# Rounding weights while the first batch is filtered: another interleaving in a spectral mixing + SwiGLU kernel

## The chip, the cores and the metric

The kernel runs on one core of a Trainium2 chip. The metric is the device time of one execution in microseconds (us). The engines are TensorE (PE, with its weight loads PEld), VectorE (DVE), ScalarE (ACT), GpSimd (Pool) and SyncE (SP, which here only issues DMAs; ACT issues some too). Each engine works through its own instructions strictly in the program's order, so an instruction that waits holds up all that stand behind it on its engine.

## The reference, cut to what matters

```python
batch, seq, dim = (8, 3008, 256)          # n_tokens = 24064, d_model = 256, d_ff = 1536
def _attn_ref(x, filt_r, filt_i):
    X = np.fft.rfft(x, axis=1)
    Y = X * (filt_r + 1j * filt_i)[None, :, :]
    return np.fft.irfft(Y, n=x.shape[1], axis=1).astype(np.float32)

def _moe_ref(x, w_gate, w_val, w_out):    # weights are float64
    g = x @ w_gate
    silu = g * (1.0 / (1.0 + np.exp(-g)))
    return (silu * (x @ w_val) @ w_out).astype(np.float32)
```

A real FFT along the sequence, a product with a filter, the inverse FFT, then a gated feed-forward block on every token. The three weight matrices come as float64, so each value arrives as two 32-bit words.

## The kernel before

The FFT is a product of two smaller DFTs (47 x 64) done as matmuls: stage 1 (`wpa`/`pa`), a transposition for the first batch (`wpt`), stage 2a (`wpb`: second DFT), the product with the filter on DVE and Pool, stage 2b (`wpc`: back), a way through DRAM (`d`), stage 3 (`wpd`/`pd`: last inverse DFT). Then 4 chunks of tokens x 3 groups of the hidden width make 12 steps of a batch, 96 in all. In a step a fast (Winograd-like) scheme makes the hidden values from sums of the sequence (`y_t`) and sums of the weights (`wt_t`, in the first batch `lent` for group 1): products `wk` (tokens P and Q of the schedule), `wa` (A, B) and `we` (E), then Silu and the product (`h`), sums of h on Pool, and the projection (`wA`, `wF`, `wG`) of the step before. In the first batch the order is three chunks for group 0 (steps 0 to 2), three for group 1 (3 to 5), three for group 2 (6 to 8), since the weights come ready one group after another. Spectral work of the next chunk or batch is mixed into the steps.

The change is in how the weights are prepared during the first batch. There are 36 halves of weight blocks (12 to each group: 8 for the hidden layer, 4 for the projection). Each half is loaded as raw 32-bit words and turned from float64 into float32 by DVE and ACT (bit masks and a scale), then Pool multiplies and combines. The numbers at the right are the line numbers by which the profile names them.

```python
    NRAW = 2
    N_EARLY = 15                       # these halves lie in places not yet used otherwise
    def load_weights(i):
        ...
        else:
            raws[i] = rpool.tile([128, 2, 128, 2], U32, ..., tag="raw", bufs=NRAW)
        queue = nc.sync if i < N_EARLY else nc.scalar
        pin(queue.dma_start(out=raws[i], in_=weights[i][0]))            # L272

    def round_half(i):
        ...
        w = rpool.tile([128, 2, 128], FP32, ..., tag="w", bufs=2)
        pin(v.tensor_scalar(out=man, in0=high, ...bitwise_and))         # L285 DVE
        pin(nc.scalar.activation(out=w, in_=man, func=AF.Copy, ...))    # L287 ACT
        yield
        pin(v.tensor_scalar(out=pw, in0=high, ...shift, and))           # L289 DVE
        pin(nc.scalar.activation(out=pf, in_=pw, func=AF.Relu, ...))    # L292 ACT
        load_weights(i + NRAW - 1)
        yield
        pin(nc.scalar.activation(out=pf, in_=pf, func=AF.Relu, ...))    # L296 ACT
        pin(nc.scalar.activation(out=pw, in_=pf, func=AF.Copy, ...))    # L297 ACT
        yield
        pin(v.scalar_tensor_tensor(out=pw, in0=raw[..1], in1=pw, ...))  # L300 DVE
        yield
        pin(v.scalar_tensor_tensor(out=w, in0=raw[..0], in1=w, ...))    # L304 DVE
        yield
        # then products and sums on Pool: L312 (projection), L323, L324, L224, L227
```

`preparing()` puts the yields of all halves in one line, with a half's Pool part inside the next half, and one weight combination a tick behind a group's last hidden half. `preparation.tick(step, n)` takes n pieces of it. Where ticks stand in the first batch:

```python
        for u in range(8):
            spec.stage1_first(u)
            if u > 3:
                preparation.tick(0, 2 + u % 2)
        ...
        for u in range(N_TWO + lag):                  # N_TWO = 12, lag = 3
            if u < N_TWO:
                spec.turn(u + 2)
                run(spec.stage2a(u))                  # matmul, 3 DVE products, 1 Pool addition
                preparation.tick(0, 1 + u % 2)
                spec.real_part(u + 1)                 # ACT copies the filter's real part, L564
                preparation.tick(0)
            if u >= lag:
                run(spec.stage2b(u - lag))
        ...                                           # loads for stage 3 (all rows)
        preparation.tick(0, 14)
        warm()                                        # idle matmuls that keep the clock up
        for step in range(4):
            run(spec.stage3(0, step))
    for d in (2, 1, 3):                               # sums of the sequence at distance d
        combine_sequence(spec.y[0], d, nc.vector if d == 1 else nc.gpsimd)
    ...
            for place, token in enumerate(SCHEDULE):
                if b == 0 and this and place * TICKS % len(SCHEDULE) < TICKS:   # TICKS = 24 a step
                    preparation.tick(step)
```

In stage 2a, the three DVE products of a tile (L548 or L551, L552, L555) read the matmul's result in PSUM; L555 releases the Pool addition `pt + qt` (L224, `room`).

Of the kernel before, what the change touches and what calls it, by code (L numbers as in the profile page):

```python
# [58 lines left out]
NH = 4  # L59
# [85 lines left out]
def kernel(  # L145
# [58 lines left out]
    off_t = cpool.tile([128, 1], FP32)  # L204
    top_t = cpool.tile([128, 1], FP32)
    nc.vector.memset(off_t, -896.0)
    nc.vector.memset(top_t, 255.0)
# [52 lines left out]
    raws = {}  # L260
    NRAW = 2
    N_EARLY = 15

    def load_weights(i):
        if i in raws or i >= len(weights):
            return
        if i < N_EARLY:
            raws[i] = early_raw(i)
        else:
            raws[i] = rpool.tile([128, 2, 128, 2], U32, name=f"raw_{i}", tag="raw", bufs=NRAW)  # L270
        queue = nc.sync if i < N_EARLY else nc.scalar
        pin(queue.dma_start(out=raws[i], in_=weights[i][0]))  # L272

    def round_half(i):
# [4 lines left out]
        pw = rpool.tile([128, 2, 128], U32, name=f"pw_{i}", tag="pw", bufs=3)  # L279
        w = rpool.tile([128, 2, 128], FP32, name=f"w_{i}", tag="w", bufs=2)  # L280
        man = w.bitcast(U32)
# [4 lines left out]
                            op0=ALU.bitwise_and))  # L286
        pin(nc.scalar.activation(out=w, in_=man, func=AF.Copy, scale=2.0 ** -20, bias=1.0))  # L287
        yield
        pin(v.tensor_scalar(out=pw, in0=high, scalar1=20, scalar2=0x7FF,  # L289
                            op0=ALU.logical_shift_right, op1=ALU.bitwise_and))  # L290
        pf = pw.bitcast(FP32)
        pin(nc.scalar.activation(out=pf, in_=pw, func=AF.Relu, bias=off_t))  # L292

        load_weights(i + NRAW - 1)
        yield
        pin(nc.scalar.activation(out=pf, in_=pf, func=AF.Relu, bias=top_t, scale=-1.0))  # L296
        pin(nc.scalar.activation(out=pw, in_=pf, func=AF.Copy, scale=-(2.0 ** 23),  # L297
# [11 lines left out]
        if use == "proj":  # L309
            j, l = at  # L310
            dst = wo_t[:, j]
            pin(e.tensor_tensor(out=dst[:, ts(l, 2), :], in0=w, in1=pf, op=ALU.mult))  # L312
            if l:
                b11, b12, b21, b22, t1, t2, t4 = [dst[:, i] for i in range(7)]
                pin(sub(e, t1, b12, b11))
                pin(sub(e, t2, b22, t1))
                pin(sub(e, b12, b22, b12))
                pin(sub(e, t4, b21, t2))
            return
# [3 lines left out]
        pin(e.tensor_tensor(out=y, in0=w[:, 1], in1=pf[:, 1], op=ALU.mult))  # L323
        pin(e.tensor_tensor(out=x if KS[i] else u, in0=x, in1=pf[:, 0], op=ALU.mult))  # L324
        if KS[i] == -1:
            pin(sub(e, u, x, y))
        elif KS[i]:
            pin(add(e, u, x, y))
            if KS[i] == 2:
                pin(add(e, u, u, y))  # L330

    def combine_weights(g, i, j):

        d = j - i
        wt_f = weights_of(0, 0, g).rearrange("p s z f -> p s (z f)")
        m = wt_f[:, SLOT[f"A{i}{j}"]]
        ui, uj, yi, yj = [wt_f[:, SLOT[f"{p}{q}"]] for p in "PQ" for q in (i, j)]
        if d == 1:
            pin(negated_sum(m, ui, uj))
        else:  # L340
            pin(add(nc.vector, m, ui, uj))
            pin(nc.scalar.mul(m, m, -1.0 / d))
        pin(sub(nc.gpsimd, wt_f[:, SLOT[f"B{i}{j}"]], yi, m))
        pin(add(nc.gpsimd, wt_f[:, SLOT[f"E{i}{j}"]], yj, m))
# [9 lines left out]

    def preparing():


        late = None
        for i in range(len(weights)):
            use, *at = weights[i][1]  # L360
            if use == "hid":
                window = (0, 0, 3)[at[0]], (0, 3, 6)[at[0]]
            else:
                window = 0 if at[0] < 2 * JB else 3, (1, 4, 7)[at[0] // JB]
            half = round_half(i)
            for n in range(5):
                yield window
                if n == 2 and late:
                    next(late, None)
                next(half)  # L370
            late = half
            if use == "hid" and at[1:] == [BLOCKS[-1], 1]:
                yield window
                next(late, None)
                for pair in PAIRS_USED:
                    yield window
                    combine_weights(at[0], *pair)
        yield window
        next(late, None)

    class Preparation:
        def __init__(self):
            self.steps = preparing()
            self.window = next(self.steps)

        def tick(self, step, n=1):
            for _ in range(n):
                if self.window and self.window[0] <= step:
                    self.window = next(self.steps, None)

        def finish(self, step):
            while self.window and self.window[1] <= step:
                self.window = next(self.steps, None)

    preparation = Preparation()
    TICKS = 24

# [20 lines left out]
    class Spectral:  # L418
# [58 lines left out]

        def load_t4(self, k, i):
            if self.b == 0 and k == 0:

                t = f0[0:NK, ts(i, NH), :]
                for r in (slice(0, NK - 16), slice(NK - 16, NK)):
                    self.load(out=t[r], in_=self.d2_rows[r, ts(i, NH), :])
            else:
                t = t4pool.tile([NK, NH, C], FP32, name=f"t4_{self.b}_{k}_{i}", tag="t4")
                self.load(out=t, in_=self.d2_rows[:, ts(2 * k + i, NH), :])
            self.t4[k, i] = t
# [78 lines left out]
        def stage2b(self, u):  # L566
# [8 lines left out]
            pin(nc.scalar.copy(out=g, in_=ps))  # L575
            queue = nc.scalar if self.b else nc.sync
            pin(queue.dma_start(out=self.twos(self.d2, u), in_=g))
# [39 lines left out]

    def combine_sequence(y, d, v=nc.gpsimd):

        n = 4 - d  # L620
        yb, yv = y[:, 0:4], y[:, 4:8]
        first = SUM[f"A0{d}"]
        pa, pb, pe = [y_t[:, first + 6 * e:first + 6 * e + n] for e in range(3)]
        pin(add(v, pa, yv[:, 0:n], yv[:, d:4]))
        if d == 1:
            pin(sub(v, pe, pa, yb[:, 0:n]))
            pin(add(v, pb, pa, yb[:, d:4]))
            return
        for dst, src, f in ((pe, yb[:, 0:n], -d), (pb, yb[:, d:4], d)):
            pin(nc.scalar.mul(dst, src, float(f)))  # L630
            pin(add(v, dst, dst, pa))
# [155 lines left out]
    with tc.tile_pool(name="start", bufs=1) as spool0:  # L787
# [22 lines left out]
        def early_raw(i):  # L810
            t = wt_t[:, spare[i]:spare[i] + 2].rearrange("p s z f -> p (s z f)") if i < 8 else \
                wo_f[:, JB * 7 * 128 + 512 * (i - 8):JB * 7 * 128 + 512 * (i - 7)]
            return t.bitcast(U32).rearrange("p (b f two) -> p b f two", b=2, two=2)

        unit_t = spool0.tile([128, 128], FP32, name="unit")
        pin(nc.scalar.dma_start(out=unit_t, in_=unit_dram.ap()))
        pin(nc.vector.memset(zero, 0.0))
        idle(zero, [bank("idle") for _ in range(5)], 512)
        pin(nc.sync.dma_start(out=wf_t, in_=wf_dram.ap()))
# [6 lines left out]
        for u in range(8):  # L826
# [3 lines left out]
            if u > 3:  # L830
                preparation.tick(0, 2 + u % 2)
        for i in range(8, N_EARLY):
# [4 lines left out]
        for u in range(N_TWO + lag):  # L837
            if u < N_TWO:
                spec.turn(u + 2)
                run(spec.stage2a(u))  # L840
                preparation.tick(0, 1 + u % 2)
                spec.real_part(u + 1)
                preparation.tick(0)
            if u >= lag:
                run(spec.stage2b(u - lag))
        for i in range(2):
            spec.load_t4(0, i)
        for i in range(2):
            spec.load_t4(1, i)
        following = Spectral(1)  # L850
        for u in range(2):
            following.load_x(u)
        preparation.tick(0, 14)
        warm()
        for step in range(4):
            run(spec.stage3(0, step))
    for d in (2, 1, 3):
        combine_sequence(spec.y[0], d, nc.vector if d == 1 else nc.gpsimd)

# [52 lines left out]
    def chore(step, token, f, *args):  # L912
        chores.setdefault((step, token), []).append((f, args))

    for step in range(NT):
        for d, token in ((2, "Q2"), (1, "A01"), (3, "Q3")):
# [10 lines left out]
    for g, step in ((0, 1), (1, 3), (2, 6)):  # L927
        for piece, token in enumerate(("B02", "B12", "A23", "B23")):
            chore(step, token, keep_weights, g, piece)

    for b in range(B):
# [33 lines left out]
        for step in range(NCHUNK * NG + (b == B - 1)):  # L965
# [17 lines left out]
            for place, token in enumerate(SCHEDULE):  # L983
                if b == 0 and this and place * TICKS % len(SCHEDULE) < TICKS:
                    preparation.tick(step)
# [64 lines left out]
```

## Time and profile before

| | |
|---|---|
| time, median of 3 runs | 3009.26 us (3007.68 to 3009.94) |
| span of the profiled execution | 3004.9 us |
| PE busy | 2938.8 us (98%) |
| DVE, ACT, Pool busy | 65%, 54%, 53% |
| mean granted clock of TensorE | 0.991 |

"Busy" counts time in which an engine has an instruction in work; PE can be busy and yet slow when the granted clock is below 1. The last part of a line of a timeline, in brackets, is the time that the engine stood idle before the instruction, and what ended it. A table of stretches has, in this order: the stretch in us from the start, its length, busy time (and instructions) of PE, PEld, DVE, ACT and Pool, the mean granted clock, the DMA engines' busy share, and GB/s. The first chunk's steps begin at 97.0, 136.7, 171.4, 208.3, 252.4, 283.3, 322.6 us (the first `f<-wk` of each).

### The profile page before, as it was taken

The numbers are of one execution on the slowest core, as the hardware profiler recorded it, in microseconds if no ns is written. First come the engines' busy times: TensorE is split into PE (matmuls) and PEld (weight loads), VectorE is DVE, ScalarE is ACT, GpSimd is POOL, SyncE is SP. The second block draws the span as 40 slices with busy tenths as digits, with TensorE's granted clock in tenths as the row PEclk, the third lists the DMA queues.
The fourth block names the chain that finished last, engine by engine and source line by source line (L and its number), as shares of the span: only waits on it lengthen the run. The fifth ranks groups of instructions, "written<-read, shape, count | busy, mean of one in ns | idle before, by whom it ended". The sixth has DMA issues, their size and how long they took to land.

```text
span 3004.9 us, 57645 instructions
## 1 busy us (share of the span) xinstructions
PE 2938.8 (98%) x20286; PEld 2838.2 (94%) x20286; DVE 1939.4 (65%) x4380; ACT 1615.8 (54%) x4207; POOL 1583.5 (53%) x1763
## 2 busy tenths in 40 slices
PE   7798999999999999999999999999999999999999
PEld 5787899999999999999999999999999999999999
DVE  7766776566765666557665576655776566766665
ACT  5566445555555555555555545555545555555554
POOL 3675465445645555545545555545555445554453
PEclk9899999999999999999999999999999999999999
DMA  7467684656655656456655575556664566644442
GB/s 204 130 208 256 226 281 155 191 186 205 198 170 175 215 180 209 154 191 204 197 177 186 172 230 178 182 175 193 200 211 158 184 193 195 199 160 145 139 136 89
DMA packets 217082, 558.60 MB, mean 186 GB/s; under 512 B 29872, under 2 KB 107552, under 8 KB 216512
## 3 DMA queue, kind: packets, MB, share of 16 engines
q1 hardware_dynamic: 167354, 481.13, 50.1%
q10 hardware_dynamic: 40512, 49.89, 5.0%
q0 software_dynamic: 8928, 23.89, 2.6%
q8 instruction: 163, 2.67, 0.4%
q14 instruction: 125, 1.02, 0.1%
HBM read 459.73 MB, written 95.05 MB: 185 GB/s over the span
## 4 chain that ended last, share of the span: by engine, by line
PE 89%; POOL 1%; DMA 1%; DVE 1%; ACT 1%; issue 0%; ACTq 0%; SPq 0%; DVEq 0%; POOLq 0%
PE wa L679 23%; PE wA L758 16%; PE wk L679 15%; PE we L679 12%; PE wG L758 8%; PE wF L758 4%; PE pd L587 3%; PE pa L499 3%; PE pc L571 2%; PE pb L539 2%; DMA raw<-in_moe_w_val_dram 0%; POOL h L227 0%; DVE o L224 0%; DMA lent<-in_filt_r_dram 0%; POOL wt_t L224 0%
## 5 line engine op out<-in xcount | busy, mean ns | idle before, releaser
L679 PE MATMUL wa<-y_t,wt_t 128*128 128x188 f32 x4464 | 884.2, 324 | 12.0 <-POOL wo_t L227 3.9
L679 PEld LDWEIGHTS wa<-y_t,wt_t 128*128 128x128 f32 x4464 | 733.6, 191 | 37.6 <-issue 18.4
L224 POOL TENSOR_TENSOR h<-h 128x376 f32<-128x376 f32 x190 | 183.3, 985 | 790.1 <-DVE h L726 790.1
L758 PE MATMUL wA<-wo_t,h 128*128 128x128 f32 x4608 | 580.0, 276 | 6.8 <-DVE o L224 5.0
L758 PEld LDWEIGHTS wA<-wo_t,h 128*128 128x128 f32 x4608 | 564.6, 192 | 22.2 <-issue 11.5
L679 PE MATMUL wk<-y,wt_t 128*128 128x188 f32 x2976 | 571.1, 325 | 4.2 <-ACT f L694 2.7
L227 POOL TENSOR_TENSOR h<-h 128x376 f32<-128x376 f32 x570 | 555.0, 995 | 0.5
L679 PEld LDWEIGHTS wk<-y,wt_t 128*128 128x128 f32 x2976 | 482.0, 191 | 29.8 <-issue 19.8
L227 DVE TENSOR_TENSOR we<-we,m 128x376 f32<-128x376 f32 x576 | 318.7, 556 | 196.7 <-PE we L679 140.4
L679 PE MATMUL we<-y_t,wt_t 128*128 128x188 f32 x2232 | 432.4, 323 | 0.0
L679 PEld LDWEIGHTS we<-y_t,wt_t 128*128 128x128 f32 x2232 | 370.5, 190 | 0.0
L227 POOL TENSOR_TENSOR D<-f,f 128x376 f32<-128x376 f32 x288 | 280.2, 986 | 118.7 <-ACT f L694 118.0
L231 DVE SCALAR_TENSOR_TENSOR y<-wk,c 128x376 f32<-128x376 f32 x480 | 245.2, 543 | 143.6 <-ACT we L710 88.8
L714 ACT COPY m<-wa 128x376 f32<-128x376 f32 x576 | 271.6, 472 | 88.4 <-PE wa L679 87.5
L758 PE MATMUL wG<-wo_t,h 128*128 128x128 f32 x2304 | 288.3, 275 | 0.6 <-DVE o L224 0.6
L721 ACT ACTIVATE g<-wa 128x188 f32<-128x188 f32 x576 | 187.6, 326 | 187.8 <-PE wa L679 181.0
L758 PEld LDWEIGHTS wG<-wo_t,h 128*128 128x128 f32 x2304 | 281.4, 192 | 0.8 <-DVE o L224 0.8
L721 ACT ACTIVATE u<-we 128x188 f32<-128x188 f32 x576 | 188.8, 328 | 166.1 <-DVE we L227 146.0
L694 ACT ACTIVATE f<-wk 128x376 f32<-128x376 f32 x288 | 139.3, 484 | 234.8 <-PE wk L679 213.9
L698 ACT COPY c<-wk 128x376 f32<-128x376 f32 x288 | 135.9, 472 | 225.7 <-PE wk L679 225.7
L701 DVE SCALAR_TENSOR_TENSOR x<-wk,f 128x376 f32<-128x376 f32 x192 | 104.5, 544 | 225.8 <-PE wk L679 225.1
L710 ACT COPY we<-y 128x376 f32<-128x376 f32 x480 | 223.6, 487 | 30.8 <-DVE h L726 13.2
(127 smaller groups left out, 3952.4 us busy)
## 6 DMA issues: line engine op xcount, KB each, us to landing
wt_t<-w_all SPq DMA_DIRECT2D x174, 896.0 KB
wt_t<-w_all SPq DMA_DIRECT2D x174, 768.0 KB
t<-d SPq DMA_DIRECT2D x62, 384.0 KB
d<-t ACTq DMA_DIRECT2D x112, 192.0 KB
lent<-de_tbl SPq DMA_DIRECT2D x84, 256.0 KB
lent<-in_filt_r_dram SPq DMA_DIRECT2D x336, 64.0 KB
lent<-d SPq DMA_DIRECT2D x84, 256.0 KB
d<-lent ACTq DMA_DIRECT2D x84, 256.0 KB
```

The lines of the kernel that those rows point to most:

```text
L224: return eng.tensor_tensor(out=dst, in0=a, in1=b, op=ALU.add)
L227: return eng.tensor_tensor(out=dst, in0=a, in1=b, op=ALU.subtract)
L231: return nc.vector.scalar_tensor_tensor(out=dst, in0=a, scalar=-1.0, in1=b, op0=ALU.mult, op1=ALU.subtract)
L499: pin(nc.tensor.matmul(out=ps[0:NK], lhsT=wf_t, rhs=self.x.pop(u), start=True, stop=True))
L679: pin(nc.tensor.matmul(out=ps[:, z], lhsT=self.wt[:, SLOT[p], z], rhs=rhs, start=start and z == 0, stop=True, skip_group_check=True))
L694: pin(act.mul(self.small(f"f{i}", f"f{i}", 1), t[f"k{i}"], -1.0))
L698: pin(act.copy(out=self.small(f"c{i}", f"c{i}", 1), in_=t[f"k{i}"]))
L701: pin(v.scalar_tensor_tensor(out=dst, in0=t[f"k{j}"], scalar=-1.0, in1=t[f"f{i}" if j == 3 else f"D{at}"], op0=ALU.mult, op1=ALU.add))
L710: pin(act.copy(out=self.bank(f"e{at}"), in_=t[f"y{at}"]))
L714: pin(act.copy(out=self.small(f"m{at}", "m", 4), in_=t[f"a{at}"]))
L721: pin(act.activation(out=self.small(op, "g", 3, 1)[:, 0], in_=ps[:, 1], func=AF.Silu))
L758: pin(nc.tensor.matmul(out=self.tiles[at][:, t, :], lhsT=self.hs[i][:, HID[p], t0:t0 + 128], rhs=wo_t[:, JB * q + i, WO[p], :], start=star ...
```

## The change

It moves the preparation's instructions, so that they wait less for each other and for loads. Six things are done at once: in the filter's stage the rounding comes between the second and third DVE product of a tile, with Pool's part held until the addition has been issued; every piece gets a tick of its own in a fixed table (a half every 4 ticks, its pieces at ticks 0, 1, 2, 3, 6, 7, 9, 10, and 20 ticks a step); raw halves may also lie in parts of `wo_t` that are written last, so that five places rotate, and are asked for ten ticks ahead where the place is free; the sums of the sequence are made in another order, partly by DVE; the rows of `d` that come last are loaded last, and the last two stores go by ACT's queue; idle matmuls are put behind the first inverse, and the Silu table is loaded at the start. Stores of the prepared weights are spread over two steps instead of one.

```diff
-    NRAW = 2
-    N_EARLY = 15
+    N_LENT = 4 * (NG - 1) * (2 + JB // 2) + 8          # 32
+    def spot_of(i):
+        spot = (i - N_EARLY) % 5
+        return spot if i < N_LENT and spot < 3 else None
+    N_EARLY = 12
...
+        elif spot_of(i) is not None:
+            raws[i] = bits(4 * 7 * 128 + 512 * spot_of(i))      # in wo_t
         else:
-            raws[i] = rpool.tile(..., tag="raw", bufs=NRAW)
+            raws[i] = rpool.tile(..., tag="raw", bufs=2)
...
-        w = rpool.tile([128, 2, 128], FP32, ..., bufs=2)
+        if i % 3 == 2 and i < N_LENT:
+            w = ...                                             # a third place, in wo_t
+        else:
+            w = rpool.tile([128, 2, 128], FP32, ..., bufs=2)
...
         pin(v.tensor_scalar(out=man, in0=high, ...))
-        pin(nc.scalar.activation(out=w, in_=man, func=AF.Copy, ...))
         yield
         pin(v.tensor_scalar(out=pw, in0=high, ...))
+        pin(nc.scalar.activation(out=w, in_=man, func=AF.Copy, ...))
+        yield
         pin(nc.scalar.activation(out=pf, in_=pw, func=AF.Relu, bias=off_t))
-        load_weights(i + NRAW - 1)
+        pin(nc.scalar.activation(out=pf, in_=pf, func=AF.Relu, bias=top_t, scale=-1.0))
         yield
-        pin(nc.scalar.activation(out=pf, in_=pf, func=AF.Relu, bias=top_t, scale=-1.0))
         pin(nc.scalar.activation(out=pw, in_=pf, func=AF.Copy, ...))
...
+            for i, (_, (use, *at)) in enumerate(weights):
+                gap = 4 if i != 2 * len(BLOCKS) and i != len(weights) - 2 else 8
+                b = base[-1] + gap if i else 0
+                if i >= N_EARLY:
+                    same = [n for n in range(N_EARLY, i) if spot_of(n) == spot_of(i)]
+                    k = 2 if spot_of(i) is None else 1
+                    last = base[same[-k]] + 8 if same[k - 1:] else 0
+                    put(max(last, b - 10), lambda i=i: load_weights(i), by)
+                for n, t in enumerate((0, 1, 2, 3, 6, 7, 9, 10)):
+                    put(b + t, go, by, n > 5)
+                # weight combinations: three ticks each, one begun a tick, from b + 11
...
-    TICKS = 24
+    TICKS = 20
...
+        pin(nc.scalar.activation(out=one, in_=off_t, func=AF.Silu))
...
-                run(spec.stage2a(u))
-                preparation.tick(0, 1 + u % 2)
+                step = spec.stage2a(u)
+                next(step)
+                next(step)                                      # matmul, two DVE products
+                preparation.tick(0, 2, hold=True)
+                run(step)                                       # third product, Pool's addition
+                preparation.release()                           # Pool's part of the ticks
                 spec.real_part(u + 1)
-                preparation.tick(0)
             if u >= lag:
                 run(spec.stage2b(u - lag))
+            if u == N_TWO:
+                for i in range(2):
+                    spec.load_t4(0, i, 0)                       # rows 0 to 79
         for i in range(2):
-            spec.load_t4(0, i)
+            spec.load_t4(0, i, 1)                               # the last 16 rows
...
-        preparation.tick(0, 14)
+        preparation.finish(0)
         warm()
         for step in range(4):
             run(spec.stage3(0, step))
+        idle(zero, [bank("idle") for _ in range(3)], 512)
-    for d in (2, 1, 3):
-        combine_sequence(spec.y[0], d, nc.vector if d == 1 else nc.gpsimd)
+    for d in (2, 1):
+        combine_sequence(spec.y[0], d, va=nc.vector)            # first sum on DVE, rest on Pool
+    chore(0, "P0", lambda: combine_sequence(cur.y[0], 3))
...
-        for piece, token in enumerate(("B02", "B12", "A23", "B23")):
-            chore(step, token, keep_weights, g, piece)
+        for piece in range(len(PIECES)):
+            chore(step + piece // 2, ("B02", "E23")[piece % 2], keep_weights, g, piece)
```

## The prediction

> **What bounds the kernel now.** I read the page's first part first, for the bound, then busy time by stretch, cut where each (sequence, weight group) step of the first batch begins, then the waits before matmuls in that stretch, and last the timelines of the engines that end those waits.
>
> ```profile
> PE 2938.8 (98%) x20286; PEld 2838.2 (94%) x20286; DVE 1939.4 (65%) x4380; ACT 1615.8 (54%) x4207; POOL 1583.5 (53%) x1763
> ```
>
> TensorE is the bound: 66 us of the 3004.9 us span are not busy. All that the change touches lies in the first batch, so the next question is how much of those 66 us lies there. The columns of the table are the stretch, its length, busy time of PE, weight loads, DVE, ACT and Pool, the granted clock, DMA share and GB/s.
>
> ```profile
> 28.80:79.50 50.70, 30.59 (x126) 23.01 (x124) 47.77 (x64) 29.51 (x60) 24.29 (x28) 0.87 0.66 184
> 79.50:97.00 17.50, 15.98 (x77) 13.82 (x77) 11.65 (x18) 8.30 (x19) 13.14 (x19) 0.81 0.59 160
> 97.00:136.70 39.70, 30.54 (x145) 28.03 (x145) 28.70 (x59) 24.27 (x63) 24.76 (x32) 0.78 0.34 119
> 136.70:171.40 34.70, 32.36 (x220) 31.34 (x220) 25.68 (x60) 25.11 (x68) 25.90 (x35) 0.95 0.67 219
> 171.40:208.30 36.90, 32.38 (x218) 30.92 (x217) 25.70 (x60) 23.83 (x66) 27.78 (x39) 0.95 0.49 158
> 208.30:252.40 44.10, 36.17 (x207) 31.99 (x206) 24.64 (x58) 23.73 (x65) 18.05 (x25) 0.88 0.75 258
> 252.40:283.30 30.90, 29.57 (x191) 26.79 (x191) 24.99 (x60) 22.03 (x60) 17.59 (x28) 1.00 0.74 244
> 283.30:322.60 39.30, 32.30 (x198) 27.24 (x197) 26.46 (x61) 21.70 (x58) 24.53 (x32) 1.00 0.59 186
> 417.80:448.00 30.20, 30.20 (x210) 29.68 (x210) 22.79 (x50) 14.66 (x40) 19.04 (x24) 1.00 0.83 279
> ```
>
> The last row is a later step that runs at PE's pace: 30.2 us, no idle. Rows three to eight are steps 0 to 5, and they take 39.7, 34.7, 36.9, 44.1, 30.9 and 39.3 us. Nearly all idle PE time of the whole run is in the rows above 322.6, and on top of it the clock is down to 0.78 to 0.95 in five of them. With a loss of (1 - clock) x PE busy, step 0 loses 0.22 x 30.54 = 6.7 us and step 3 0.12 x 36.17 = 4.3 us beside 9.2 and 7.9 us of idle. In the first row DVE is busy 47.77 of 50.70 us: there, and only there, DVE is the bound.
>
> What fills DVE there is seen in its timeline: the same instruction takes 0.28 us when Pool rests and 1.37 us when Pool has an addition running.
>
> ```profile
> 24.57 0.28 DVE L289 TENSOR_SCALAR pw<-wt_t 128x256 uint32<-128x256 uint32 x1
> ...
> 48.14 1.37 DVE L289 TENSOR_SCALAR pw<-wt_t 128x256 uint32<-128x256 uint32 x1
> ```
> ```profile
> 47.98 1.37 POOL L224 TENSOR_TENSOR room<-room,y_t 128x512 f32<-128x512 f32 x1 [1.39 <-DVE y_t L555]
> ```
>
> The addition starts at 47.98, just after L555 has given it its input, the second DVE instruction behind L555 runs into it. In the steps the picture is another one: DVE stands still until a raw weight half has come from DRAM, and PE stands still behind it.
>
> ```profile
> 215.62 0.29 DVE L285 TENSOR_SCALAR w<-raw 128x256 uint32<-128x256 uint32 x1 [5.48 <-DMA raw<-in_moe_w_out_dram]
> ...
> 240.62 0.29 DVE L285 TENSOR_SCALAR w<-raw 128x256 uint32<-128x256 uint32 x1 [4.54 <-DMA raw<-in_moe_w_val_dram]
> ```
> ```profile
> 216.89 1.62 PE L679 MATMUL wa<-y_t,lent 128*128 128x188 f32 x4 [2.77 <-DVE wa L701]
> ...
> 241.79 1.62 PE L679 MATMUL wa<-y_t,lent 128*128 128x188 f32 x4 [5.11 <-ACT wa L705]
> ```
>
> **What the Trainium skill says.** SBUF — State Buffer, section "Who interferes with whom": DVE and GpSimd share a pair of ports under an exclusive lock held for a whole instruction, and DVE takes it in its two-port modes or with two SBUF inputs. The trace agrees: 1.37 instead of 0.28 us beside Pool's 1.37 us. TensorE: Matmul & The Clock Gate, section "What's actually happening": an idle window of about 3.4 us halves the clock, and a busy window brings it back. The trace agrees in kind: four wa records take 1.62 us right after the gaps above and 0.80 us elsewhere. ScalarE: Activation LUTs, section "What ACT_TABLE_LOAD costs": about 1283 ns for a load; here the one before the first Silu took 1.28 us, at 107.17, in step 0.
>
> **The change, part by part.** I number the halves of the weights 0 to 35, twelve to a group.
>
> 1. Rounding between the filter's products. The instructions that collide (L285, L289, L300, L304) now stand between the second and the third DVE product of a tile, and Pool's rounding products are held until after Pool's addition. Before, one of each pair of rounding instructions took 1.36 to 1.50 us, twelve times in this stretch: 12 x 1.07 = 12.8 us. Now the addition of the tile before (1.37 us) runs beside two products that read PSUM (2 x 0.69 = 1.4 us) and is about over when rounding comes. The held Pool products (0.45 us each, 1.5 per tile) can still be met: 12 x 0.4 = 5 us stay. Gain 8 us.
>
> 2. The end of the filter: last rows of the inverse loaded last, the last two stores on ACT's queue. The 28 idle matmul records that follow the last filter product run from 80.70 to 88.84, and the inverse starts at 88.67, right behind them, so earlier rows are hidden there: 0. The three new idle matmuls of 512 columns behind the inverse cost PE about 3 x 0.95 = 2.9 us (four records, two matmuls, took 1.91 us) where 1.52 us were idle: they delay by 1 us net, and should keep the clock up.
>
> 3. Sums in another order. In step 0, PE waited 3.88 us before its first wa product, at 105.31, behind Pool's weight products; DVE had been held 1.69 us there for a buffer. Now DVE makes the two sums that are read first, the third distance comes later, and no projection half's products stand ahead of them. The table load (1.28 us) moves into the start, where ACT waits for input anyway. Step 0 has 9.2 us idle and 6.7 us of clock to win; dependences inside the first step, which has no projection of an older step to fill it, keep about half. Gain 8 us.
>
> 4. Ticks and more places. In place of two raw buffers and a load asked for about half a half ahead, there are five places and a load ten ticks ahead: 10 of 20 ticks in a 30 us step, 15 us, against 4.6 to 9.1 us to landing (issued 307.45, used 312.04; issued 231.40, used 240.62). The DMA waits of steps 1 to 3 go away. Step 3: 44.1 - 30.2 = 13.9 us lost; I take 11 back. Steps 1 and 2: 3.8 and about 6 us lost, of which Pool's weight combinations keep the larger part (Pool is busy 27.78 of 36.90 us in step 2); gain 3.5 us.
>
> 5. A new wait. The lent places end with half 31. Half 32 must use a raw buffer, which is free only 8 ticks after half 30 began, and that is the tick in which half 32 itself begins: in the new program its load is issued directly ahead of the instruction that reads it, and the same for half 33. Both fall in step 4. Each holds DVE for at least 4.6 us, as in step 3 before, where two such waits (5.48 and 4.54 us) cost nearly 12 us with the clock. With somewhat more slack around them I put step 4 at 8 us more: loss 8 us.
>
> 6. Step 5 lost 39.3 - 28.5 = 10.8 us, with one extraction piece fewer than a full step; there Pool makes the last group's twelve combinations among the sums of h. They stay, a little more spread: gain 4 us. Steps 6 to 8: 1 us.
>
> The sum is -8 + 1 - 8 - 3.5 - 11 + 8 - 4 - 1 = -26.5 us: 3009.3 - 26.5 = 2982.8, say 2983 us. From step 9 on nothing changes.
>
> **Rivals.** First: Pool takes DVE's place as the bound. Pool is busy 24.29 of 50.70 us in the filter and at most 27.78 of 36.90 in a step, so it has room on average; but its combinations come in one block, and products behind a block keep DVE's buffers. If Pool is what really sets steps 0, 2 and 5, parts 3 and 6 bring little: 2995 us. Second: the new DMA waits of part 5 cost more than those of step 3 did, because two stores of weights start in the same step, and they pull the clock down too: 14 instead of 8 us, 2989 us. Third, on the good side: all waits in the first batch hang on one another through the clock; once DVE no longer stalls, PE stays at full rate and nearly all loss of steps 0 to 3 and half of the rest goes away. The ceiling of that is some 60 us of idle and about 20 us of clock; half of it gives 2969 us, two thirds 2956 us. Fourth: the filter is hardly shortened, since ACT (29.51 us busy, plus what it waits for DVE) or the arrival of the filter's tables takes over: 8 us less gain, 2991 us.
>
> **Range and chances.** The single parts are uncertain by 3 to 6 us each and partly hang together; 2964 to 2998 us holds four cases in five. Two per cent are 60 us, which would need nearly all of the ceiling: 4%. A loss of 60 us would need a new stall of a size that no part here can make: 1%.
>
> **What would show it.** Right, if the stretch of the filter is shortened by about 8 us with no rounding instruction of DVE over 1 us in it; if the first wk product comes near 87 us and step 0 takes about 32 us with the clock above 0.9; if step 3 takes about 33 us without a DVE wait for a raw half; if step 4 is the one that has become longer, with two DVE waits of 4 us or more for the w_out halves. Wrong, if Pool or ACT ends the waits in the filter, if the load of half 32 is hidden, or if steps 0 and 5 keep their length.

## The result, and the profile after

The changed kernel takes 2985.88 us (median of 4, 2984.88 to 2988.16) against 3009.6 us before in the same session: ratio 0.9922, 95% interval 0.9905 to 0.9939. The page's first line of the changed kernel:

```profile
PE 2932.4 (98%) x20292; PEld 2832.4 (95%) x20292; DVE 1929.5 (65%) x4379; ACT 1616.7 (54%) x4207; POOL 1584.0 (53%) x1764
```

51 us of the 2983.5 us span are not busy, where it was 66. The table of stretches, cut at the steps of the changed kernel:

```profile
28.80:73.00 44.20, 30.36 (x126) 22.50 (x124) 36.55 (x66) 29.98 (x61) 21.98 (x28) 0.88 0.82 203
73.00:89.60 16.60, 16.43 (x77) 12.85 (x77) 12.72 (x21) 9.09 (x21) 14.91 (x23) 0.90 0.76 197
89.60:119.10 29.50, 23.91 (x140) 21.64 (x138) 21.95 (x54) 22.33 (x61) 21.71 (x28) 0.94 0.50 167
119.10:152.90 33.80, 31.35 (x222) 30.07 (x222) 29.09 (x61) 25.72 (x70) 28.32 (x36) 1.00 0.63 208
152.90:188.00 35.10, 31.94 (x223) 30.11 (x223) 31.63 (x66) 24.43 (x67) 31.40 (x43) 1.00 0.67 212
188.00:219.50 31.50, 30.87 (x200) 27.82 (x198) 22.49 (x55) 24.43 (x66) 17.26 (x24) 1.00 0.88 304
219.50:265.50 46.00, 36.06 (x199) 32.35 (x200) 29.32 (x68) 23.48 (x64) 20.79 (x30) 0.85 0.63 209
265.50:302.60 37.10, 32.51 (x197) 29.96 (x196) 24.98 (x55) 18.58 (x50) 25.30 (x35) 0.91 0.49 157
396.30:426.60 30.30, 30.30 (x211) 29.78 (x210) 22.82 (x50) 14.73 (x41) 18.91 (x24) 1.00 0.78 261
```

Row by row against before: step 0 begins at 89.6 instead of 97.0 us; steps 0 to 5 take 29.5, 33.8, 35.1, 31.5, 46.0 and 37.1 us instead of 39.7, 34.7, 36.9, 44.1, 30.9 and 39.3; steps 6 to 8 together 1.5 us less; step 9 begins at 396.3 instead of 417.8 and is as long as it was. All of the gain lies ahead of step 9. One step, step 4 (219.5 to 265.5), has become 15.1 us longer.

In the filter, DVE is busy 36.55 of 44.20 us now. Its rounding instructions, in the timeline of the changed kernel, and Pool's additions on both sides of them:

```profile
47.89 0.42 DVE L317 SCALAR_TENSOR_TENSOR pw<-wt_t,pw 128x256 uint32<-128x256 uint32 x1
48.24 0.43 DVE L321 SCALAR_TENSOR_TENSOR w<-wt_t,w 128x256 f32<-128x256 uint32 x1
48.70 0.69 DVE L607 TENSOR_TENSOR y_t<-wpb,f 64x512 f32<-64x512 f32 x1
...
51.56 0.29 DVE L303 TENSOR_SCALAR wo_t<-wt_t 128x256 uint32<-128x256 uint32 x1
51.77 0.29 DVE L306 TENSOR_SCALAR pw<-wt_t 128x256 uint32<-128x256 uint32 x1
```
```profile
45.86 1.27 POOL L225 TENSOR_TENSOR room<-room,y_t 128x512 f32<-128x512 f32 x1 [1.33 <-DVE y_t L607]
47.09 0.46 POOL L341 TENSOR_TENSOR wt_t<-wo_t,pw 128x128 f32<-128x128 f32 x1
...
49.52 1.28 POOL L225 TENSOR_TENSOR room<-room,y_t 128x512 f32<-128x512 f32 x1 [1.57 <-DVE y_t L607]
```

The additions run from 45.86 and 49.52, while DVE reads PSUM; the rounding comes at 47.89 and 51.56, and takes 0.29 to 0.43 us. One slow rounding instruction is left, of 1.49 us at 71.91, behind the last tile's products.

DVE is busy 11.2 us less in this row (36.55 against 47.77 us), but the row is only 6.5 us shorter, because DVE now waits for ACT: 5.7 us in all between 28.8 and 77.8, against 1.4 us before (3.1 to 3.5 us in four other runs with the same filter). ACT's copy of the filter's real part (L616), which the first product of the next tile needs, stands behind ACT's part of the rounding (L308), and that waits for the DVE instruction that now comes between the products:

```profile
44.90 0.42 ACT L308 ACTIVATE w<-w 128x256 f32<-128x256 uint32 x1 [2.14 <-DVE w L303]
45.22 1.23 ACT L616 COPY y_t<-f 64x512 f32<-64x512 f32 x2
46.48 0.69 DVE L600 TENSOR_TENSOR room<-wpb,y_t 128x512 f32<-128x512 f32 x1 [0.70 <-ACT y_t L616]
```

Behind the filter, the first wk product of step 0, before and after the change:

```profile
93.90 1.62 PE L679 MATMUL wk<-y,wt_t 128*128 128x188 f32 x4 [1.52 <-DVE y L224]
88.76 0.80 PE L731 MATMUL wk<-y,wt_t 128*128 128x188 f32 x4
```

In step 4 the waits stand where they were expected, DVE first, then PE behind it:

```profile
246.84 0.29 DVE L303 TENSOR_SCALAR w<-raw 128x256 uint32<-128x256 uint32 x1 [7.51 <-DMA raw<-in_moe_w_out_dram]
...
257.78 0.29 DVE L303 TENSOR_SCALAR w<-raw 128x256 uint32<-128x256 uint32 x1 [6.09 <-DMA raw<-in_moe_w_out_dram]
```
```profile
248.11 1.62 PE L731 MATMUL we<-y_t,lent 128*128 128x188 f32 x4 [6.40 <-DVE we L232]
258.95 1.62 PE L731 MATMUL we<-y_t,lent 128*128 128x188 f32 x4 [2.95 <-ACT we L762]
```

The load was issued at 238.97, 2.1 us behind a store of weights (236.88), and used at 246.84: 7.9 us. The four records behind the gap take 1.62 us instead of 0.80: the clock is down, to 0.85 over the step.

### The profile page after: what moved, and what is told of

Same layout as the page of the kernel before. It is cut to its first block, busy times and chain, and to the rows that moved or that the text cites. A ratio compares the mean times of both kernels' runs of the same rounds, so it can differ in the third digit from the quotient of the medians.

```text
span 2983.5 us, 57655 instructions
## 1 busy us (share of the span) xinstructions
PE 2932.4 (98%) x20292; PEld 2832.4 (95%) x20292; DVE 1929.5 (65%) x4379; ACT 1616.7 (54%) x4207; POOL 1584.0 (53%) x1764
## 4 chain that ended last, share of the span: by engine, by line
PE 89%; DMA 0%; DVE 0%; SPq 0%; issue 0%; ACT 0%; POOL 0%; ACTq 0%; DVEq 0%
PE wa L731 23%; PE wA L810 16%; PE wk L731 15%; PE we L731 12%; PE wG L810 8%; PE wF L810 4%; PE pd L639 3%; PE pa L551 3%; PE pc L623 2%; PE pb L591 2%; DMA lent<-de_tbl 0%; DMA y<-y 0%; DVE o L225 0%; POOL D L228 0%; SPq L695 0%
```

## The experiments

All are edits of the changed kernel unless another is named, and none leaves out any part of the computation. Differences between kernels are given as medians; where they are under 5 us, the stretches of the profile have to decide, since the interval of a ratio is about 0.0016 (5 us) to either side. A stretch is that of one execution.

### Step 4: lead or traffic

```diff
     def spot_of(i):
+        if N_LENT <= i < N_LENT + 2:
+            return i - N_LENT + 1          # halves 32, 33: lent places 1 and 2, free 8 ticks ahead
```

> The changed kernel, with halves 32 and 33 in two lent places that are free 8 ticks before they are needed, instead of in the raw buffers. Lead theory: the two DVE waits of step 4 (7.51 and 6.09 us) are gone, step 4 falls from 46.0 to 31-34 us, the clock stays at 1.00 there, and the time falls by 10 to 15 us, to 2971-2976 us. Rival (traffic: the two stores of weights in step 4 and the form of the w_out rows make these loads late whenever they are asked for): waits of 4 us or more stay, gain under 5 us.

2972.68 us (2971.2 to 2974.11), ratio to before 0.9876 (0.9859 to 0.9892): 13.2 us less than the changed kernel. Step 4 and step 5 of it:

```profile
218.30:250.70 32.40, 31.36 (x200) 27.87 (x199) 27.59 (x65) 23.43 (x63) 19.25 (x28) 1.00 0.84 269
250.70:287.20 36.50, 31.11 (x197) 28.35 (x196) 26.62 (x57) 18.51 (x49) 26.80 (x37) 0.95 0.56 182
```

Step 4 takes 32.4 us at full clock, and no DVE wait for a load is left in it (the longest is 1.1 us, for PE). The two loads are issued at 224.68 and 230.82, while two stores of weights still start in this step, at 235.38 and 243.86. The lead theory holds.

```diff
-        for piece in range(len(PIECES)):
-            chore(step + piece // 2, ("B02", "E23")[piece % 2], keep_weights, g, piece)
+        for piece, token in enumerate(("B02", "B12", "A23", "B23")):
+            chore(step, token, keep_weights, g, piece)
```

> The changed kernel, with the stores of the prepared weights all in one step again (as before the change), so that none falls in step 4 beside the late loads. Lead theory: the loads of halves 32 and 33 are still asked for when they are needed; the two DVE waits shorten from 7.5 and 6.1 us to the 4.6 us of a quiet load at best, time 0 to 5 us less. Rival (traffic): the two waits fall under 2 us and step 4 to 35 us or less, time 10 us less.

2982.35 us (2979.77 to 2983.35), 3.5 us less. The two waits of step 4, without stores of weights near them:

```profile
243.10 0.29 DVE L303 TENSOR_SCALAR w<-raw 128x256 uint32<-128x256 uint32 x1 [4.72 <-DMA raw<-in_moe_w_out_dram]
...
251.68 0.29 DVE L303 TENSOR_SCALAR w<-raw 128x256 uint32<-128x256 uint32 x1 [3.76 <-DMA raw<-in_moe_w_out_dram]
```

4.72 and 3.76 us instead of 7.51 and 6.09, and step 4 takes 38.5 us. The waits do not fall under 2 us, as the traffic alone would have it, but the traffic has its part: without the stores the same late loads cost 7.6 us against the 30.9 us of the kernel before (38.5 - 30.9), the size that the prediction had taken; the stores make it 15.1. A load asked for in time removes nearly all of both. Of the 7.5 us that step 4 gains here, 1.7 us are lost again in step 5 and 1.4 us in steps 6 to 8.

### The filter: the shared port

```diff
-                step = spec.stage2a(u)
-                next(step)
-                next(step)
-                preparation.tick(0, 2, hold=True)
-                run(step)
-                preparation.release()
+                run(spec.stage2a(u))
+                preparation.tick(0, 2)
```

> The changed kernel, with the two ticks of rounding behind all of a tile's work, Pool's addition included, instead of between the second and third product. Port theory: the rounding instructions of DVE run into Pool's addition again, about twelve of them take 1.3 to 1.5 us in the filter, the last filter product of DVE ends about 6 us later (near 77.5 instead of 71.5 us) and the time rises by 5 to 8 us. Rival (the gain in the filter comes from the new spacing of the pieces): DVE instructions stay short, time within 2 us of the changed kernel.

2991.73 us (2991.11 to 2993.76), 5.9 us more. The timeline shows the collision back, DVE above and Pool below:

```profile
48.68 0.29 DVE L303 TENSOR_SCALAR w<-wt_t 128x256 uint32<-128x256 uint32 x1
48.89 1.36 DVE L306 TENSOR_SCALAR pw<-wt_t 128x256 uint32<-128x256 uint32 x1
```
```profile
48.73 1.37 POOL L225 TENSOR_TENSOR room<-room,y_t 128x512 f32<-128x512 f32 x1 [1.81 <-DVE y_t L607]
```

Twelve rounding instructions of DVE take over 1.2 us in the filter, as before the change, and the last product of the filter on DVE ends at 77.66 us instead of 71.53. So the place of the rounding is what gained here, and not the new spacing. The runs show the collision and its cost; that what is shared is a port rests on the page that the prediction names.

```diff
 # the kernel before
-                run(spec.stage2a(u))
-                preparation.tick(0, 1 + u % 2)
+                step = spec.stage2a(u)
+                next(step)
+                next(step)
+                preparation.tick(0, 2 + u % 2)
+                run(step)
                 spec.real_part(u + 1)
-                preparation.tick(0)
```

> The kernel before, with one part of the change alone: the ticks of rounding stand between the second and third product of a tile, without holding Pool's part. Port theory: no more than two rounding instructions of DVE over 1.2 us in the filter, the last stage 2b product ends 5 to 8 us earlier (80.9 us before), and since the steps behind it are the old ones the time falls by about as much, 4 to 8 us. Rival (Pool's rounding products, now ahead of Pool's addition, delay it as much as the port did): gain under 2 us.

3003.37 us (2999.84 to 3008.81), ratio to before 0.9974 (0.9965 to 0.9982). The filter and step 0 of this run:

```profile
28.80:74.60 45.80, 32.00 (x131) 24.07 (x130) 37.38 (x66) 29.47 (x61) 24.65 (x33) 0.88 0.82 223
88.20:128.00 39.80, 28.10 (x142) 25.81 (x141) 28.28 (x59) 24.16 (x63) 24.77 (x32) 0.83 0.34 120
```

One part of the change alone, without holding Pool's part: one slow instruction is left, the last stage 2b product ends at 74.6 instead of 80.9 us, step 0 begins 8.8 us earlier (88.2). So the place between the products carries the gain of the filter, and in this kernel it does so without the holding. The slow instruction is again behind the last tile, at 71.91. Step 0 stays at 39.8 us: its gain has another source. In this execution 4.7 of the 8.8 us are lost again in step 8 (35.7 instead of 31.0 us), where ACT waits 4.4 us for a transfer; the last section comes back to it.

### Steps 1 to 3: lead, traffic, spacing

```diff
-                    put(max(last, b - 10), lambda i=i: load_weights(i), by)
+                    put(max(last, b - 3), lambda i=i: load_weights(i), by)
```

> The changed kernel, with raw halves asked for 3 ticks ahead instead of 10; places and spacing stay. Lead theory: 3 ticks are about 4.6 us, as short as the fastest load; DVE waits for raw halves come back in steps 1 to 3 and 5, step 3 rises from 31.5 to 36-42 us, the time rises by 8 to 20 us. Rival (places and the spacing of the pieces made the gain, not the lead): steps 1 to 3 within 2 us, time within 3 us.

2988.26 us (2986.03 to 2989.78): 2.4 us more, far less than expected, and step 3 takes 34.0 us, not 36 to 42. A DVE wait of 4.16 us is in step 3, and PE mostly does not follow it. The theory that the lead gave the whole gain of step 3 falls. The next run adds the old stores (both edits above):

> The changed kernel, with a lead of 3 ticks and the stores of a group's weights all in one step. The short lead alone cost 2.4 us, with one DVE wait of 4.16 us in step 3; the old stores alone cost nothing in step 3. Theory (the 13.9 us that step 3 lost before the change needed both: a load asked for late, and the stores of 3.3 MB in its way): waits of 6 us or more in step 3, step 3 at 37 us or more against 34.0 with the short lead alone. Rival (spacing and places made the gain of step 3, whatever the traffic): step 3 at 35 us or less.

2986.01 us (2983.61 to 2989.65); step 3 takes 37.4 us, step 4 38.4. The longest DVE waits of step 3, with the short lead alone and with the old stores too:

```profile
217.17 0.29 DVE L303 TENSOR_SCALAR w<-wo_t 128x256 uint32<-128x256 uint32 x1 [4.16 <-DMA wo_t<-in_moe_w_val_dram]
```
```profile
220.16 0.29 DVE L303 TENSOR_SCALAR w<-wo_t 128x256 uint32<-128x256 uint32 x1 [5.10 <-DMA wo_t<-in_moe_w_val_dram]
```

Against 31.5 us in the changed kernel, the short lead costs 2.5 us in step 3, the old stores nothing (31.3 us), both together 5.9 us: late loads and stores act through each other. The waits of 6 us or more did not come, though. Of the 12.6 us that step 3 gained, 5.9 are shown to be lead and traffic; the rest goes with what these two runs keep, the spacing of the pieces, the third place of `w` and the five places, and which of these it is was not tried.

### Step 0: sums, idle matmuls, table, halves ahead

```diff
-    for d in (2, 1):
-        combine_sequence(spec.y[0], d, va=nc.vector)
+    for d in (2, 1, 3):      # distance 1 on DVE, 2 and 3 on Pool, all ahead of step 0
...
-    chore(0, "P0", lambda: combine_sequence(cur.y[0], 3))
```

> The changed kernel, with the sums of the sequence in the old order (distances 2, 1, 3; distance 1 all on DVE, the others on Pool, the third ahead of step 0). Theory of the prediction (order and engine of the sums gave half of step 0): the first wa product waits again 3 us or more for Pool's sum, half-clock windows follow, step 0 rises from 29.5 to 33-36 us, time 4 to 7 us more. Rival (it was the clock, kept up by the idle matmuls, and the projection halves that no longer stand ahead): step 0 within 1.5 us, time within 2 us.

2984.1 us (2982.89 to 2986.35), step 0 28.9 us: no loss in it. It begins at 92.5 instead of 89.6 us, but not for the sums: PE waited 1.97 us for rows ahead of the inverse, and the inverse ran at half clock, its 32 records in 6.26 instead of 3.78 us. The order of the sums is not what shortened step 0.

```diff
-        idle(zero, [bank("idle") for _ in range(3)], 512)
```

> The changed kernel, without the three idle matmuls behind the first inverse. Prediction's step: they cost 1 us net and keep the clock up; without them the first wk product comes 0 to 2.5 us earlier, but a half-clock window or two fall into step 0, which rises by 2 to 6 us; time 0 to 4 us more. Rival (they only take PE's time): time 1 to 2.5 us less.

2985.88 us, the same time. The profile says why: step 0 begins 1.8 us earlier, at 87.8, and takes 2.9 us more.

```profile
87.80:120.30 32.50, 24.08 (x132) 22.08 (x131) 25.30 (x56) 22.42 (x63) 22.53 (x29) 0.89 0.45 152
```

The clock is 0.89 instead of 0.94; with a loss of (1 - clock) x PE busy that is 1.2 us. The rest is not the clock: the first wa product that waits in this step starts at about the same time in both kernels (97.40 and 97.77), so what PE gains at the start it mostly waits there, 3.66 instead of 1.75 us. The idle matmuls keep the clock up, and cost what they bring.

```diff
-        pin(nc.scalar.activation(out=one, in_=off_t, func=AF.Silu))
```

> The changed kernel, without the early Silu, so that the table is loaded before the first Silu in step 0. Theory: 1.28 us stand on ACT's path in step 0, time 0.7 to 2 us more. Rival (ACT has slack there): time within 0.5 us.

2985.96 us (2983.71 to 2986.16): no difference in the time. Step 0 takes 30.5 instead of 29.5 us in the profile, so up to 1 us of cost there cannot be excluded.

```diff
         preparation.finish(0)
+        preparation.tick(0, 8)
         warm()
```

> The changed kernel, with 8 more ticks taken ahead of step 0, so that two more projection halves stand ahead of the first sums, as before the change. Theory (step 0 gained because no projection half stands ahead of the sums on DVE, ACT and Pool): step 0's start moves 2 us or more later, PE waits 3 us or more in the first wa products and step 0 with its start together lose 4 to 8 us. Rival (the clock and the pieces' spacing made it): start and step 0 together within 2 us.

2990.85 us (2987.96 to 2997.31), 5.0 us more. The cost lies ahead of step 0: it begins at 94.3 instead of 89.6 us and takes 30.6 instead of 29.5, together 5.8 us. This adds work rather than restoring the old order: 11 halves are begun ahead of step 0 in the changed kernel, 10 in the kernel before, and 13 here (counted by their first DVE instruction). The wait is not the one expected, but that of the first product for the inverse's results, which DVE and ACT write behind the rounding:

```profile
92.62 1.59 PE L731 MATMUL wk<-y,wt_t 128*128 128x188 f32 x4 [4.03 <-DVE y L225]
```

### Two tries at a faster version

```diff
 # the kernel of e1_places
-        for i in range(8, N_EARLY):
-            load_weights(i)
...
+            if 6 <= u < 6 + N_EARLY - 8:
+                load_weights(u + 2)
```

> The kernel of the places for halves 32 and 33, and the four early loads of w_out halves asked for on SP's queue behind the first stores of the filter's results instead of ahead of them. In the changed kernel ACT stood 3.31 us in the filter for a store that SP had not yet issued, PE 3.89 us behind it, and a half-clock window of 6.8 us followed. Theory: that wait is gone, the last stage 2b product ends 2 to 4 us earlier, time 2 to 5 us under the 2972.7 us of the places alone. Rival (DVE and PE make it up before the inverse, or the loads now come too late for halves 8 to 11): within 1.5 us.

2973.23 us, no difference. ACT's wait for the store is gone, but PE's gap at the same place stays, 2.42 us, and the kernel of the places had 2.40 us there without this edit: of the 3.89 us of the changed kernel's profile, 1.5 us were one execution's timing of stores, not a fixed cost.

```diff
 # the kernel of e9_raws_later
-                            put(b + 11 + n + t, lambda c=c: next(c, None), by, t == 2)
+                            put(b + 11 + n * (1 + (g > 0)) + t, lambda c=c: next(c, None), by, t == 2)
```

> The same as the run before, and the weight combinations of groups 1 and 2 begun every second tick instead of every tick. Theory (Pool's block of twelve combinations holds the sums D and the buffers of steps 2 and 5): steps 2 (35.1 us) and 5 (36.5 us) fall by 1.5 us or more each, time 3 us or more less than the run before. Rival (the work on Pool is the same, only moved): both steps within 1 us, time within 1.5 us.

2971.86 us (2971.01 to 2974.0), 1.4 us less, within the uncertainty. Steps 4 and 5:

```profile
223.00:257.70 34.70, 32.62 (x200) 29.11 (x199) 25.55 (x62) 22.42 (x60) 20.67 (x31) 0.95 0.83 271
257.70:289.40 31.70, 30.21 (x197) 27.12 (x196) 25.41 (x54) 18.21 (x50) 23.95 (x32) 1.00 0.63 203
```

Step 5 falls from 37.4 to 31.7 us, and DVE's waits for Pool in it from 7.0 to 2.4 us, so Pool's block of combinations was most of what held it. But step 2 stays at 35.1 us, and step 4 rises by 2.3 us, with a new DVE wait of 4.15 us that the profile puts on Pool. What the spread gives in one step is partly given back in the one before it. This and the kernel of the places (0.9871 and 0.9876 of the time before) are both faster than the changed kernel (0.9922).

## Why the prediction was right

2983 us was predicted, 2985.88 us measured. The chain of reasons holds in the large, but the sum (26.5 us, measured 23.7) came as near as it did partly by luck: step 4 cost 7 us more than predicted, steps 0 and 3 brought 4 us more, and in the filter and in step 0 right totals came from wrong terms.

- **Filter (predicted 8 us, and 1 us back).** Start of step 0 7.4 us earlier against 7. The mechanism is shown from both sides: undone in the changed kernel it costs 5.9 us, done alone in the kernel before it moves step 0's start by 8.8 us. The terms were others. The last stage 2b product ends 6.4 us earlier (74.55 instead of 80.90), not 8. The 5 us that were to stay from Pool's held products did not stay; the 5.7 us of DVE's waits for ACT took their place. So the fourth rival came true in part, and ACT ending DVE's waits in the filter had been named as a sign of being wrong. Behind the filter, the first wk product comes only 5.1 us earlier (88.76; near 87 was predicted), because the new idle matmuls take 2.77 us where 1.52 us were idle; the other 2.3 us lie between that product and ACT's first `f`, where PE ran at half clock before.
- **The rows loaded last (predicted 0).** In the changed kernel the inverse still starts right behind the idle matmuls. In the run without the later idle matmuls those took 6.81 us at full clock, and PE then waited 1.84 us for the rows: with the clock up, the load is the bound there. Most of the other runs of the changed program show such a wait too, up to 2.4 us.
- **Step 0 (predicted 8 us).** 10.2 us measured, but not for the reasons given: the order of the sums is worth nothing, the table load at most 1 us, and the third reason did not hold, since one more half is begun ahead of step 0 than before and Pool makes a projection product ahead of the sums (at 86.01). Start and step 0 together are better compared, because what is saved in one can be waited for in the other: step 1 begins 17.5 us earlier (119.1 instead of 136.7). The filter's interleaving is worth 8.7 us of it when it is done alone and 9.3 when it is undone, the idle matmuls about 1. The remaining 7 us or so came with the pieces' spacing or the places of `w`; neither was run alone, so that stays open.
- **Steps 1 and 2 (3.5 us), step 3 (11 us).** 2.7 and 12.6 us. Lead and traffic are shown for 5.9 us of step 3; the prediction had put all of it on the DMA waits.
- **Step 4 (a loss of 8 us).** 15.1 us: this is the mis-sized term. The wait is the predicted one, at the predicted halves, and asking in time removes 13.2 us. The size that was taken is that of late loads without stores beside them, as the run with the old stores shows. The second rival named the stores and 14 us; it was right on the size.
- **Step 5 (4 us), steps 6 to 8 (1 us).** 2.2 and 1.5 us. Pool's combinations hold step 5, as the first rival had it; spreading them helped in no other step. The 28.5 us that the prediction took for a step 5 without losses come from no measurement: in the run with the spread PE is busy 30.21 us of it at full clock.
- **A reading.** The clock is down in six rows of the prediction's table above 322.6, not in five. Nothing rests on the count.

## What to carry to other kernels

Where DVE and Pool take turns on the same data, put DVE instructions that read PSUM, not those that read SBUF, beside Pool's instruction: here this was worth 6 us, without removing any work. Then look at what the third engine has behind that work: here ACT's next copy came late by it. When buffers rotate, look at the ends of the rotation: two halves that fell back on the old buffers undid 13 us. A late load took 7.9 us with a store of weights just ahead of it and 5.1 us in the run without (237.96 to 243.10), so compute the lead from a transfer beside others, and check in the program's order that each load really is issued that far ahead.

## What the runs showed of the hardware

The clock can go to half after gaps shorter than had been expected. In the kernel before, PE stood 2.33 us before a wk product at 147.52, and 3.4 us of half clock began 0.7 us later; in the changed kernel 3.4 us of it followed a gap of 1.75 us:

```profile
97.77 2.87 PE L731 MATMUL wa<-y_t,wt_t 128*128 128x188 f32 x8 [1.75 <-DVE wa L753]
```

Eight records took 2.87 us there, and 1.44 to 1.54 us elsewhere. The Trainium skill, TensorE: Matmul & The Clock Gate, section "What's actually happening", speaks of an idle window of about 3.4 us; here shorter gaps did it, and the measurement decides. Nor does the length of a gap decide alone: before the inverse, 2.37 us of waiting in the run with the raw loads later were followed by half clock 2 us later (its 32 records took 5.26 us), and 2.34 us in the run with the late table were not (3.78 us). What else decides was not tried.

In step 8, ACT waited for a sequence chunk to come back from DRAM, in the changed kernel for 2.96 us, in kernels that got there with other timing for up to 4.7 us, with PE waiting 1.4 to 2.8 us behind it, while the kernel before had no PE wait there over 0.5 us. So part of an earlier start was lost again at this transfer. What holds it up was not tried.

```profile
387.75 0.92 ACT L682 ACTIVATE y_t<-y 128x376 f32<-128x376 f32 x2 [2.96 <-DMA y<-y]
```
